# A fused attention, MLP and soft-MoE kernel: softmax over the slots at the end, row-tiled fp32 combine, smaller VectorE work, free slots handed out in any order

## Chip, cores and metric

The kernel runs on one core of a Trainium2 chip. The metric is device microseconds (us) of one execution, the median of several; smaller is better. "Engines" are PE (TensorE; PEld its weight loads), DVE (VectorE), ACT (ScalarE), POOL (GpSimd) and SP, which issues every DMA here from one queue.

## What is computed

Three layers in fp32, on 4608 tokens (8 batches of 576) of width 512. In the code `SP` = 72 pooled keys, and one *tile* is 128 tokens (36 tiles).

```
# 1 attention, 8 heads of 64, keys and values pooled by 8
k_p, v_p = mean over 8 tokens of k, v
x = softmax(q k_p^T / 8) v_p
# 2 MLP with a rational activation, 512 -> 2048 -> 512
h = x w_in;  P = a0 + a1 h + a2 h^2 + a3 h^3;  Q = 1 + |b0||h| + |b1|h^2
x = (P/Q) w_out
# 3 soft mixture of 8 experts with 4 slots each
logits = x phi                                  # 4608 x 32
slot_in = softmax over TOKENS(logits)^T x       # 32 x 512
slot_out[e] = relu(slot_in[e] w1[e]) w2[e]      # per expert, 512 -> 1024 -> 512
out = softmax over SLOTS(logits) slot_out       # 4608 x 512
```

## The kernel before

**Order of the work.** Each step of the program is an `op(engine, duration, function, reads, writes, key)`. `Plan.run` (line 146) plays a list schedule: of all steps whose inputs are there and whose buffers can be had, it takes the one that can start first by the durations written beside it, then the one with the smallest `key`. Each engine, and SP's DMA queue, then executes its instructions strictly in the order in which they were picked. `LAT = 0.12` is added where a result goes to another engine. So the constants set only the order; on the chip an instruction whose input is late holds up all that stands behind it on its engine.

**Buffers.** `Res` (line 40) is a ring of equal buffers under a tag: the next user gets the buffer that was given out longest ago, and waits for it even where another one is already free. Tags that matter here: `kv` (3, raw weights and keys/values from DMA), `t` (2, a weight matrix row block while it is rebuilt), `gt` (10, MLP activations transposed), `w` (16, the MLP's first weights), `xh` and `xl` (2 each, attention output split in a high and a low part), `h` (2, PSUM, 2 banks each) and `wk` (2, PSUM). A buffer made while `late` is set (everything of the experts and the tail) gets a slot only after all earlier users of the tag have had theirs.

**First stage.** Weights come as 64-bit numbers and are rebuilt in fp32 by `words` (line 394): a DMA to `raw`, ACT at L401, then four VectorE steps L402 to L407. `win` (line 410) then splits `w_in` into a high (ACT L416) and a low part (POOL L417). `wout` (line 420) stores the rebuilt rows to DRAM (L424), transposes them and multiplies with phi to get `wpt`, so that logits come straight from the activations. `pooling` (line 296) sums keys and values over 8 tokens on VectorE (L303 keys, 2 per batch; L310 values, 4 per batch).

**Rounds.** 9 rounds of 4 tiles. In a round, `dense` (line 449) runs over 8 pairs of 128 hidden units: 24 fp32r matmuls of 512 columns (L458 to L460) into `h`; the activation on ACT (L465 to L468, L475, L478), POOL (L469, L472, L474) and DVE (L470, L479 to L483); then `lg` (L490, logits) and `gp` (L503, transposes) on PE and copies to `gt` (L507). Beside it `attention` (line 315) prepares the next round's 4 tiles; its row sums are a reduce, an addition of 1e-9 (L355) and a reciprocal. At the end of a round `routing` (line 511) takes the maximum per slot over tokens (reduce L518, transpose L520, DVE L523 to L525, PE L528), the exponentials, rescales the running sum of slot inputs (PE L572, DVE L578), and also makes this round's softmax over slots (DVE L554 to L564, ACT L558).

**Experts and tail.** `experts` (line 586) queues the 64 weight DMAs of 512 KB (`wx`) and 16 of 256 KB. `tail` (line 620) finishes the slot inputs, runs layer one (L694) and layer two (L723), both 4 experts side by side in the four 32-column groups of PE, then the combine: slot outputs are split in a high and a low part (L761 ACT, L762 DVE), for each tile the slot weights stand four times over 128 rows (POOL L733, PE L741, ACT L749, DVE L753), and one fp32r matmul per tile (L772) gives 128 x 512 outputs, two tiles per `h` buffer. ACT copies the first tile out (L774), DVE the second (L776), and one DMA of 512 KB stores both (L777).

Of the kernel before, what the change touches and what calls it, by code (L numbers as in the profile page):

```python
# [18 lines left out]
SP = 72  # L19
# [17 lines left out]
LAT = 0.12  # L37


class Res:  # L40


    def __init__(self, pool, tag, bufs):
        self.pool, self.tag, self.bufs, self.given = pool, tag, bufs, []
        self.due = 0

    def free_at(self, late, more):
        n = len(self.given) + more
        if late and self.due:
            return None  # L50
        if n < self.bufs:
            return 0.0
        n -= self.bufs
        return self.given[n].released() if n < len(self.given) else None


class Buf:
# [13 lines left out]
    def released(self):  # L71
        return self.end if self.left == 0 else None

    def choose(self, more={}):
        best = None
        for r in self.res:
            f = r.free_at(self.late, more.get(r, 0))
            if f is not None and (best is None or f < best[0]):
                best = (f, r)
        return best  # L80

    def take(self):
        r = self.choose()[1]
        r.given.append(self)
        r.due -= not self.late
        self.t = r.pool.tile(self.shape, self.dtype, tag=r.tag, name=self.name, bufs=r.bufs)
# [12 lines left out]
class Plan:  # L99
# [46 lines left out]
    def run(self):  # L146
# [14 lines left out]
        while left:  # L161
            best = None
            for t in live:
                s0 = t.ready
                ok, more = True, {}
                for b in t.bufs:
                    if b.t is None:
# [4 lines left out]
                        more[c[1]] = more.get(c[1], 0) + 1  # L172
# [12 lines left out]
            if best is None:  # L185
                raise RuntimeError("no task can start: " + str([(t.alts[0][0], t.key, [b.name for b in t.bufs if b.t is None and b.choose() is None]) for t in live]) + str({k: [(b.name, b.left) for b in r.given[-r.bufs:]] for k, r in self.R.items()}))
            _, t, i, s = best
            e, d, fn, p = t.alts[i]
            if len(t.alts) > 1:
                for i2, (e2, d2, fn2, p2) in enumerate(t.alts):  # L190
                    s2 = max(t.ready, free[e2])
                    if e2 == "POOL":
                        s2 = max(s2, port["DVE"])
                    elif e2 == "DVE" and p2:
                        s2 = max(s2, port["POOL"])
                    if s2 + d2 < s + d:
                        e, d, fn, p, s = e2, d2, fn2, p2, s2
# [25 lines left out]
def soft_moe_kernel(ctx: ExitStack, tc: tile.TileContext, qT, kT, vP, w_in, w_out, ab, phi, w1, w2, sel, vmask, out):  # L223
# [11 lines left out]
    for tag, n in (("q", 3), ("kv", 3), ("at", 2), ("att", 1), ("st", 4), ("xh", 2), ("xl", 2), ("A", 3), ("S", 2),  # L235
                   ("U", 3), ("w", 16), ("gt", 10), ("L", 1), ("en", 1), ("m", 3), ("cs", 2), ("t", 2), ("wo", 1)):
        R[tag] = Res(sb, tag, n)
    for tag, n in (("h", 2), ("r", 1), ("wk", 2)):
        R[tag] = Res(ps, tag, n)

    late = [False]
    P.R = R
# [15 lines left out]
    call = fixed([128, NTILE, 32], "call", np_=NR)  # L258
# [6 lines left out]
    vms = fixed([128, 4], "vms")  # L265
    wpt = fixed([128, NF, 32], "wpt", np_=NF)
    den = fixed([128, 1], "den")
    mrun = fixed([1, 5, 32], "mrun")
    lgb = Fixed(ps.tile([128, 2, 128], F32, name="lg"))
    lgb.np = 2  # L270
# [9 lines left out]
    op("POOL", 0.2, lambda: g_.memset(den.t, 0.0), [], [den], -90)  # L280
    op("POOL", 0.4, lambda: g_.memset(Sacc.t, 0.0), [], [Sacc], -90)
    op("POOL", 0.2, lambda: g_.memset(mrun.t[:, 4, :], -3.0e38), [], [mrun], -90)
# [7 lines left out]
    def att_key(t):  # L290
        r, j = divmod(t, 4)
        if r == 0:
            return -8.0 + 6.0 * j
        return run_at(r - 1) + run_len(r - 1) * j / 4.0

    def pooling(b):
        need = att_key(first_tile[b])
        for i in range(2):
            key = need - 0.4 + 0.1 * i if b == 0 else need - 40 + 8 * i
# [4 lines left out]
               [t], [(o, i)], key)  # L304
        for i in range(4):
            key = need + 4 + 0.1 * i if b == 0 else need - 20 + 5 * i
            t = buf("kv", [SP, 128, 8], "vst")
# [3 lines left out]
               [t], [(o, i)], key)  # L311
# [3 lines left out]
    def attention(t):  # L315
# [6 lines left out]
        if j == 0:  # L322
            xh[r] = buf("xh", [128, 4, 512], "xh", F32R, 4)
            xl[r] = buf("xl", [128, 4, 512], "xl", F32R, 4)
# [4 lines left out]
        e = buf("at", [128, 2, 4, SP], "e", np_=2)  # L329
# [14 lines left out]
        def sub(par):  # L344
            m = st.t[:, 0, 4 * par : 4 * par + 4].rearrange("p (h o) -> p h o", o=1).to_broadcast([128, 4, SP])
            v_.tensor_tensor(out=e.t[:, par], in0=v3(par), in1=m, op=ALU.subtract)
# [4 lines left out]
        op("ACT", 0.69, lambda: a_.activation(out=e.t, in_=e.t, func=AF.Exp, scale=1.0 / 64.0), [e], [e], k0 + 4)  # L351

        def sums():
            v_.tensor_reduce(out=st.t[:, 1, :], in_=e.t.rearrange("p a h s -> p (a h) s"), axis=AX.X, op=ALU.add)
            v_.tensor_scalar_add(st.t[:, 1, :], st.t[:, 1, :], 1e-9)  # L355
# [492 lines left out]
```

## Time and profile before

| what | us |
|---|---|
| runs (3) | 1035.82, 1037.12 (median), 1042.73 |
| profiled execution, its own time | 1038.82 |
| its span, first to last instruction | 1037.0 |
| mean granted TensorE clock | 0.91 of 2.4 GHz |

In the profile a line such as L469 is a line of the kernel. Busy time of PE is modelled from pipelined starts. A row of the waits says which engine and line stood idle, and whose end released it. A row of the windows gives, for a stretch of the span, each engine's busy time with the number of instructions, the granted clock (1.00 is 2.4 GHz, 0.50 is 1.2 GHz), the busy share of the 16 DMA engines and GB/s.

### The profile page before, as it was taken

The page shows a single profiled execution, that of the slowest core. Times are in us where ns is not written, and L with a number is a line of the kernel's source. Part 1 is how long each engine was busy: PE and PEld are TensorE (multiplying, and loading weights), DVE is VectorE, ACT ScalarE, POOL GpSimd, SP SyncE. Part 2 cuts the span into 40 slices and gives each one's busy share as a digit, 9 for nine tenths or more (in the row PEclk, how much of TensorE's full clock was granted, in tenths as well). Part 3 has the DMA queues.
Part 4 walks back from the last instruction along what each step waited for, and adds up shares of the span by engine and source line. Part 5 has one row for each costly group of instructions (what it writes and reads, how often), then busy time and mean ns, then how long its engine had stood idle before and what let it go on. Part 6 is the DMA issues. An engine that isn't in the chain of part 4 may idle for free. (4 is left out here: it accounts for less than half of the span.)

```text
span 1037.0 us, 15229 instructions
## 1 busy us (share of the span) xinstructions
PE 876.4 (85%) x5939; PEld 604.6 (58%) x5939; DVE 722.2 (70%) x1142; ACT 600.2 (58%) x880; POOL 498.4 (48%) x288
## 2 busy tenths in 40 slices
PE   2785686678998998898999989999999898948995
PEld 1564565456675666666767656666676675633322
DVE  5758786777966796787778887878687658552204
ACT  1454555545666657667667666776776766652203
POOL 0143433344465755656556665665675664640000
PEclk9997768788998999999999999999999998978995
DMA  7532334432310021021002100300000052345979
GB/s 221 157 92 92 112 112 117 163 94 75 116 53 1 11 78 46 11 73 40 22 1 75 59 1 21 106 11 22 1 11 2 1 165 82 124 138 221 400 280 356
DMA packets 34151, 97.54 MB, mean 94 GB/s; under 512 B 4000, under 2 KB 4128, under 8 KB 34080
## 3 DMA queue, kind: packets, MB, share of 16 engines
q1 hardware_dynamic: 34080, 96.57, 28.1%
q8 instruction: 47, 0.77, 0.3%
q14 instruction: 24, 0.20, 0.1%
HBM read 82.92 MB, written 13.63 MB: 93 GB/s over the span
## 5 line engine op out<-in xcount | busy, mean ns | idle before, releaser
L469 POOL TENSOR_TENSOR a<-a,s 128x1024 f32<-128x1024 f32 x72 | 172.3, 2394 | 264.7 <-ACT a L467 229.4
L458 PE MATMUL h<-xh,wh 128*128 128x512 f32 x576 | 261.9, 455 | 29.7 <-ACT wh L416 14.5
L460 PE MATMUL h<-xh,wh 128*128 128x512 f32 x576 | 239.9, 417 | 1.8 <-POOL wh L417 1.6
L459 PE MATMUL h<-xl,wh 128*128 128x512 f32 x576 | 239.2, 415 | 0.2 <-DVE xl L388 0.2
L474 POOL TENSOR_TENSOR u<-u,s 128x1024 f32<-128x1024 f32 x72 | 171.7, 2385 | 5.8
L479 DVE SCALAR_TENSOR_TENSOR u<-u,r 128x512 f32<-128x512 f32 x144 | 98.1, 681 | 94.3 <-ACT r L478 93.8
L458 PEld LDWEIGHTS h<-xh,wh 128*128 128x128 f32 x576 | 116.2, 202 | 69.1 <-DVE a L470 19.2
L460 PEld LDWEIGHTS h<-xh,wh 128*128 128x128 f32 x576 | 115.9, 201 | 32.6 <-POOL wh L417 5.4
L507 ACT ACTIVATE gt<-gp 128x512 f32<-128x512 f32 x144 | 82.8, 597 | 76.4 <-PE gp L503 75.8
L459 PEld LDWEIGHTS h<-xl,wh 128*128 128x128 f32 x576 | 116.5, 202 | 17.8 <-DVE xl L388 1.0
L478 ACT ACTIVATE r<-s 128x512 f32<-128x512 f32 x144 | 86.8, 603 | 48.5 <-DVE a L483 47.1
L481 DVE SCALAR_TENSOR_TENSOR r<-a,abt,r 128x512 f32<-128x512 f32 x144 | 107.8, 749 | 0.0
L483 DVE SCALAR_TENSOR_TENSOR a<-u,r 128x512 f32<-128x512 f32 x144 | 98.8, 686 | 4.3
L470 DVE SCALAR_TENSOR_TENSOR a<-h,abt,a 128x1024 f32<-128x1024 f32 x72 | 91.9, 1277 | 12.4 <-POOL a L469 12.4
L490 PE MATMUL lg<-a,wpt 128*32 128x128 f32 x1152 | 64.1, 298 | 42.0 <-DVE a L483 40.4
L465 ACT ACTIVATE s<-h 128x1024 f32<-128x1024 f32 x72 | 73.7, 1023 | 42.4 <-PE h L460 42.1
L503 PE MATMUL gp<-ident,a 128*128 128x128 f32 x576 | 91.8, 297 | 5.1 <-DVE Sacc L578 2.3
L468 ACT ACTIVATE u<-h 128x1024 f32<-128x1024 f32 x72 | 73.6, 1022 | 37.1 <-PE h L460 36.5
L475 ACT ACTIVATE s<-u,cc 128x1024 f32<-128x1024 f32 x72 | 82.7, 1149 | 14.5 <-POOL u L474 14.4
L472 POOL TENSOR_SCALAR s<-u,gb 128x1024 f32<-128x1024 f32 x72 | 86.7, 1204 | 6.5
L467 ACT ACTIVATE a<-h,abt 128x1024 f32<-128x1024 f32 x72 | 87.1, 1209 | 0.0
L503 PEld LDWEIGHTS gp<-ident,a 128*128 128x128 f32 x576 | 70.7, 151 | 25.7 <-issue 12.3
(119 smaller groups left out, 1110.1 us busy)
## 6 DMA issues: line engine op xcount, KB each, us to landing
wx<-in_w SPq DMA_DIRECT2D x64, 512.0 KB
kst<-in_kT SPq DMA_DIRECT2D x16, 576.0 KB
qt<-in_qT SPq DMA_DIRECT2D x36, 256.0 KB
vst<-in_vP SPq DMA_DIRECT2D x32, 288.0 KB
out_dram<-o SPq DMA_DIRECT2D x18, 512.0 KB
raw<-in_w_in SPq DMA_DIRECT2D x16, 512.0 KB
raw<-in_w_out SPq DMA_DIRECT2D x16, 512.0 KB
wod<-wo SPq DMA_DIRECT2D x16, 256.0 KB
```

The source lines that it names most:

```text
L458: p_.matmul(o, w[:, 0, k], xh[r].t[:, k], start=(k == 0), stop=False)
L459: p_.matmul(o, w[:, 0, k], xl[r].t[:, k], start=False, stop=False)
L460: p_.matmul(o, w[:, 1, k], xh[r].t[:, k], start=False, stop=(k == 3))
L467: op("ACT", t_act(1024, 1, 2), lambda: a_.activation(out=fl(A), in_=fl(h), func=AF.Identity, scale=a3, bias=a2), [h, abt], [A], c)
L469: op("POOL", t_pool(1024), lambda: g_.tensor_tensor(out=fl(A), in0=fl(A), in1=fl(S_), op=ALU.mult), [S_], [A], c + 3)
L470: op("DVE", t_dve(1024, 1), lambda: v_.scalar_tensor_tensor(out=fl(A), in0=fl(h), scalar=a1, in1=fl(A), op0=ALU.mult, op1=ALU.add), [h, ab ...
L474: op("POOL", t_pool(1024), lambda: g_.tensor_tensor(out=fl(U), in0=fl(U), in1=fl(S_), op=ALU.mult), [S_], [U], c + 5)
L478: op("ACT", t_act(512, 0), lambda f=f, q=q: a_.activation(out=q.t, in_=S_.t[:, f], func=AF.Exp, scale=-1.0), [(S_, f)], [q], c + 10)
L479: op("DVE", t_dve(512), lambda f=f, q=q: v_.scalar_tensor_tensor(out=U.t[:, f], in0=U.t[:, f], scalar=QC, in1=q.t, op0=ALU.add, op1=ALU.mult),
L481: op("DVE", t_dve(512, 1), lambda f=f, q=q: v_.scalar_tensor_tensor(out=q.t, in0=A.t[:, f], scalar=a0, in1=q.t, op0=ALU.add, op1=ALU.mult) ...
L483: op("DVE", t_dve(512), lambda f=f, q=q: v_.scalar_tensor_tensor(out=A.t[:, f], in0=U.t[:, f], scalar=-2.0, in1=q.t, op0=ALU.add, op1=ALU. ...
L503: p_.transpose(pt.t[:, j, f, :], A.t[:, f, o : o + 128], ident)
```

## The change

**Slots.** A tag is now a list of separate slots; a new buffer takes whichever slot is free first. Tags gain alternatives: raw weights may lie in `kv` or `gt`, rebuilt rows in `t` or `gt`, the first values in `kv` or `gt`; `xh` and `xl` become one tag `x` with 4 slots, and 8 of the expert loads use it: four as before, and four that take the last round's two buffers (items 24 to 27).

**Plan.** A step on PE is planned 0.6 us behind its inputs (`SLACK`) instead of 0.12. Pooling may run on POOL as a tree of three additions, where that starts earlier. Round 1's attention is due later, and pooling of batch 1 too.

**VectorE.** The 1e-9 of the row sums is a 73rd element of the reduced buffer, so L355 goes. In `routing`, the running maximum is put in as a 129th column of the logits by ACT (so L524 goes), the copy over four groups goes from DVE (L525) to ACT, the update of `den` from DVE (L535) to ACT; L538 goes.

**Softmax over slots.** L554 to L564 and L558 leave the rounds; a round only copies its transposed logits (one ACT copy of 128 columns). In the tail three groups (4, 4 and 1 rounds) make maximum, difference, exponential, sum and reciprocal, then PE transposes once per round instead of four times, and ACT copies. The division moves into the output copies.

**Combine.** The slot outputs are divided (ACT), gathered to four copies by an fp32 matmul of 512 columns and copied out in two halves (ACT, DVE). Each tile is one fp32 matmul with 32 rows, tile j of a round in row group j.

**Last pair.** The last pair of the last round runs its activation in halves, and its two copies to `gt` may go to DVE.

```
-LAT = 0.12
+LAT, SLACK = 0.12, 0.6
...
-    def free_at(self, late, more):
-        n = len(self.given) + more
...
-        n -= self.bufs
-        return self.given[n].released() if n < len(self.given) else None
+    def free_at(self, i):
+        b = self.held[i]
+        return 0.0 if b is None else None if b.left else b.end
...
-                o.ready = max(o.ready, t.end + (LAT if o.alts[0][0] != e or t.nbytes else 0.0))
+                f = o.alts[0][0]
+                o.ready = max(o.ready, t.end + (0.0 if f == e and not t.nbytes else SLACK if f == "PE" else LAT))
...
+    def tree(t, o):
...
+        g_.tensor_tensor(out=t[ix(0, 4)], in0=t[ix(0, 4)], in1=t[ix(4, 8)], op=ALU.add)
+        g_.tensor_tensor(out=t[ix(0, 2)], in0=t[ix(0, 2)], in1=t[ix(2, 4)], op=ALU.add)
...
+        g_.tensor_tensor(out=o, in0=t[ix1(0)], in1=t[ix1(1)], op=ALU.add)
...
-        raw = buf("kv", [128, 512, 2], "raw", I32)
+        raw = buf(["kv", "gt"], [128, 512, 2], "raw", I32)
...
-        t = buf("t", [128, 512], "wi")
+        t = buf(["t", "gt"], [128, 512], "wi")
...
-            v_.tensor_tensor(out=mrun.t[:, 4, :], in0=mrun.t[:, 4, :], in1=mrun.t[:, 0, :], op=ALU.max)
-            v_.tensor_copy(mrun.t[:, 0:4, :], mrun.t[:, 4:5, :].to_broadcast([1, 4, 32]))
...
+        op("ACT", 0.27, lambda: a_.activation(out=mrow_.t[:, 0:4, :], in_=mrow_.t[:, 4:5, :].to_broadcast([1, 4, 32]), func=AF.Copy),
+           [(mrow_, 0)], [(mrow_, 1)], k0)
...
+        op("PE", 0.9, lambda: p_.matmul(pg.t, gsel.t, so.t, start=True, stop=True), [so, gsel], [pg], kk)
+        op("ACT", 0.4, lambda: a_.activation(out=so4.t[:, 0:256], in_=pg.t[:, 0:256], func=AF.Copy), [pg], [(so4, 0)], kk)
+        op("DVE", 0.42, lambda: v_.tensor_copy(so4.t[:, 256:512], pg.t[:, 256:512]), [pg], [(so4, 1)], kk)
...
-                op("PE", 0.25, lambda t=t, pv=pv: p_.matmul(pv(), cT[t // 16].t[:, t % 16, :], spk.t, start=True, stop=True), [(cT[t // 16], t % 16 // 4), spk], [(q, j)], kk)
...
+                for i in range(2):
+                    j = 2 * (n % 2) + i
+                    rr = slice(32 * j, 32 * j + 32)
+                    p_.matmul(po.t[:, i], cTs.t[rr, n // 2, :], so4.t[rr, :], start=True, stop=True)
```

## Rows read from the trace of the kernel before

**Rows 1.** the page, busy time, share of the span and instructions

```profile
PE 876.4 (85%) x5939; PEld 604.6 (58%) x5939; DVE 722.2 (70%) x1142; ACT 600.2 (58%) x880; POOL 498.4 (48%) x288
```

**Rows 2.** windows by stage: us, busy PE, PEld, DVE, ACT, POOL, clock, DMA share, GB/s

```profile
30.00:263.00 233.00, 175.07 (x1048) 131.81 (x1048) 176.84 (x271) 120.44 (x191) 89.15 (x54) 0.82 0.38 116
...
683.00:767.00 84.00, 80.11 (x623) 57.18 (x621) 61.28 (x104) 60.56 (x89) 53.04 (x30) 0.98 0.04 10
...
935.00:1006.00 71.00, 67.45 (x390) 23.92 (x390) 13.79 (x32) 10.40 (x21) 3.93 (x7) 0.95 0.84 326
1006.00:1037.00 31.00, 17.86 (x37) 8.46 (x36) 13.11 (x19) 11.32 (x19) 0.00 (x0) 0.57 0.83 304
```

**Rows 3.** lines on DVE, first 263 us: busy us, mean ns | idle before

```profile
L310 DVE TENSOR_REDUCE vp<-vst 72x128 f32<-72x1024 f32 x12 | 14.4, 1206 | 2.5 <-DMA vst<-in_vP 2.4
L403 DVE TENSOR_SCALAR wo<-wo 128x512 int32<-128x512 int32 x16 | 14.0, 874 | 0.5
...
L402 DVE TENSOR_SCALAR wo<-wo 128x512 f32<-128x512 f32 x16 | 10.6, 663 | 18.0 <-ACT wo L401 18.0
L342 DVE TENSOR_REDUCE st<-sc 128x4 f32<-128x288 f32 x22 | 9.3, 452 | 11.8 <-PE sc L336 11.8
...
L303 DVE TENSOR_REDUCE kp<-kst 128x144 f32<-128x1152 f32 x6 | 8.1, 1353 | 11.2 <-DMA kst<-in_kT 11.2
...
L403 DVE TENSOR_SCALAR wi<-wi 128x512 int32<-128x512 int32 x16 | 6.8, 426 | 0.5
...
L355 DVE TENSOR_SCALAR st<-st 128x8 f32<-128x8 f32 x11 | 5.6, 505 | 0.4
```

**Rows 4.** waits of SP's DMA queue, first 260 us: us, times, longest us

```profile
SPq L275 <- DVE wo L407: 96.3, 13, 13.5
```

**Rows 5.** waits of PE in the rounds, 263 to 935 us: us, times, longest

```profile
PE lg L490 <- DVE a L483: 31.3, 24, 3.4
PE h L458 <- DVE a L470: 11.6, 19, 0.9
PE pm L528 <- DVE mrun L525: 8.5, 6, 3.0
```

**Rows 6.** timeline at the end of one round, DVE: start us, us

```profile
773.95 2.24 DVE L524 TENSOR_TENSOR mrun<-mrun 1x32 f32<-1x32 f32 x1
```

**Rows 7.** the same timeline, PE

```profile
776.50 0.38 PE L528 MATMUL pm<-ident,mrun 1*128 1x1 f32 x2 [1.50 <-DVE mrun L525]
```

**Rows 8.** windows in the tail and the output stage, columns as in Rows 2

```profile
932.00:935.00 3.00, 2.77 (x17) 1.85 (x17) 0.68 (x3) 1.01 (x2) 0.00 (x0) 0.50 0.00 0
947.00:950.00 3.00, 3.00 (x30) 0.82 (x22) 0.00 (x0) 0.00 (x0) 0.00 (x0) 1.00 1.03 416
955.00:962.00 7.00, 7.00 (x66) 2.54 (x59) 0.75 (x1) 0.53 (x2) 0.43 (x1) 1.00 0.83 297
...
1011.00:1031.00 20.00, 15.37 (x30) 6.99 (x28) 10.74 (x16) 9.23 (x16) 0.00 (x0) 0.50 1.03 378
```

**Rows 9.** timeline of the output stage: start us, us, engine, line

```profile
1006.05 0.69 ACT L761 ACTIVATE shi<-lo,mf 128x512 fp32r<-128x512 f32 x1 [27.74 <-PE lo L723]
1006.77 0.75 DVE L762 SCALAR_TENSOR_TENSOR spk<-lo,mf,shi 128x512 fp32r<-128x512 f32 x1 [25.94 <-ACT shi L761]
...
1012.05 2.12 PE L772 MATMUL po<-spk,cT 128*128 128x512 f32 x4 [0.52 <-DVE o L776]
...
1013.31 0.60 ACT L774 ACTIVATE o<-po 128x512 f32<-128x512 f32 x1 [1.14 <-PE po L772]
1013.94 0.69 DVE L776 COPY o<-po 128x512 f32<-128x512 f32 x1 [1.04 <-ACT o L774]
```

**Rows 10.** the page's costliest groups, one addition of 1024 columns on POOL

```profile
L469 POOL TENSOR_TENSOR a<-a,s 128x1024 f32<-128x1024 f32 x72 | 172.3, 2394 | 264.7 <-ACT a L467 229.4
```

**Rows 11.** lines, whole span: a one-column step on ACT

```profile
L534 ACT ACTIVATE m<-mold,m 128x1 f32<-128x1 f32 x8 | 2.3, 290 | 0.0
```

**Rows 12.** the chain that ended last, in layer one: start us, us

```profile
954.75 7.07 PE l L694 x64
```

More of the change, by code (lines that the diff above doesn't have):

```diff
@@ L36, with __init__, view @@
 t_pool1 = lambda n: 0.1 + 0.0011 * n
[L37 removed]
+LAT, SLACK = 0.12, 0.6
 class Res:
[L43 to L54 removed]
+    def __init__(self, pool, tag, n, width, kept=()):
+        self.pool, self.tag, self.kept = pool, tag, kept
+        self.n, self.width, self.due, self.held = n, width, 0, [None] * n
+    def free_at(self, i):
+        b = self.held[i]
+        return 0.0 if b is None else None if b.left else b.end
+    def view(self, i, shape, dtype, name):
+        if self.kept:
+            return self.kept[i]
+        n = 1
+        for x in shape[1:]:
+            n *= x
+        assert n <= self.width
+        return self.pool.tile(shape, dtype, tag=f"{self.tag}{i}", name=name, bufs=1)
 class Buf:
@@ L62, in __init__ @@
         self.res, self.late = res, late
-        if not late:
-            for r in res:
-                r.due += 1
+        for r in res:
+            r.due += not late
         self.shape, self.dtype, self.name = shape, dtype, name
@@ L69, in __init__, with choose @@
         self.w, self.r = {}, {}
-    def released(self):
-        return self.end if self.left == 0 else None
-    def choose(self, more={}):
+    def choose(self, but=()):
         best = None
         for r in self.res:
-            f = r.free_at(self.late, more.get(r, 0))
-            if f is not None and (best is None or f < best[0]):
-                best = (f, r)
+            if self.late and r.due:
+                continue
+            for i in range(r.n):
+                if (r, i) in but:
+                    continue
+                f = r.free_at(i)
+                if f is not None and (best is None or f < best[0]):
+                    best = (f, r, i)
         return best
     def take(self):
[L83 to L86, printed above, removed]
+        _, r, i = self.choose()
+        r.held[i] = self
+        for o in self.res:
+            o.due -= not self.late
+        self.t = r.view(i, self.shape, self.dtype, self.name)
 class Fixed(Buf):
@@ L185, in run @@
             if best is None:
-                raise RuntimeError("no task can start: " + str([(t.alts[0][0], t.key, [b.name for b in t.bufs if b.t is None and b.choose() is None]) for t in live]) + str({k: [(b.name, b.left) for b in r.given[-r.bufs:]] for k, r in self.R.items()}))
+                raise RuntimeError("no task can start: " + str([(t.alts[0][0], t.key, [b.name for b in t.bufs if b.t is None and b.choose() is None]) for t in live][:40]))
             _, t, i, s = best
             e, d, fn, p = t.alts[i]
[L189 to L197, printed above, removed]
             for b in t.bufs:
@@ L463, in dense @@
         A, S_, U = (buf(x, [128, 2, 512], x.lower(), np_=2) for x in "ASU")
-        fl = lambda x: x.t.rearrange("p a b -> p (a b)")
-        op("ACT", t_act(1024), lambda: a_.activation(out=fl(S_), in_=fl(h), func=AF.Square), [h], [S_], c, after=was("sq"), also=[A, U])
-        seq("sq", P.tasks[-1])
-        op("ACT", t_act(1024, 1, 2), lambda: a_.activation(out=fl(A), in_=fl(h), func=AF.Identity, scale=a3, bias=a2), [h, abt], [A], c)
-        op("ACT", t_act(1024), lambda: a_.activation(out=fl(U), in_=fl(h), func=AF.Abs), [h], [U], c)
```

249 lines of the change are left out of this document (123 added, 126 removed).

## Prediction, made before the change was run

> **What bounds the kernel now.** I read the page first: PE is busy 85% of the span and no other engine over 70% [rows 1]. Such an average hides the stages, so the windows come next [rows 2]. They show four different limits.
>
> *First stage, to 263 us.* From 30 to 263 us PE is busy 175.07 of 233 us at a clock of 0.82, DVE 176.84 us, ACT 120.44 us: nobody is full, DVE is nearest. So I asked for DVE's lines there, with the idle time ahead of each [rows 3]. The largest removable piece is 18.0 us ahead of L402, waiting for ACT's L401, which reads the raw weights. Why L401 is late shows in the DMA queue's own waits: SP stands 96.3 us in front of loads until DVE's last rebuild step L407 has let go of a raw buffer [rows 4]. That is a shortage of slots: three `kv` buffers in a ring, two `t` buffers. SP works in order, so such a load also holds up what is queued behind it. Bound: DVE's work plus waits made by slots.
>
> *Rounds, 263 to 935 us, 84 us each.* In the round shown PE is busy 80.11 of 84 us at clock 0.98, DVE only 61.28 [rows 2]. PE is the bound, and only what makes PE wait can be won. PE's waits there: 31.3 us in 24 pieces where `lg` (L490) was put in the order before its input from L483 was done, 11.6 us where `h` waits for L470 to read the last buffer, 8.5 us in the routing chain at L528 [rows 5]. The last is seen closely in one round: L524, an operation on 32 numbers, takes 2.24 us [rows 6], and PE stands 1.50 us at L528 [rows 7].
>
> *Experts, 935 to 1006 us.* DMA share 0.84 over the stage [rows 2], 1.03 at 416 GB/s once it runs, but 0.00 at 932 to 935 us when no slot is free [rows 8]. Bound: weight loading, with a hole ahead of it.
>
> *Output, from 1006 us.* DMA share 1.03 at 378 GB/s with PE's clock at 0.50 [rows 8]: 18 stores of 0.524 MB at 378 GB/s are 1.387 us each, 25.0 us together. The computing just keeps up: one pair goes through PE from 1012.05, ACT at 1013.31 and DVE at 1013.94 to 1014.63, that is 2.58 us, with two buffers in turn, 1.29 us a pair [rows 9].
>
> **The change part by part.** All against the profiled execution, whose span is 1037.0 us.
>
> *First stage.* (a) Slots: raw and rebuilt rows can take ten more slots, so loads run ahead. I count the 18.0 us ahead of L402 as gone; between 0 (SP's order keeps them late) and -18.0. (b) DVE's 11.8 us at L342 waits for PE's scores; a plan that expects PE later and attention of round 1 due later should remove half, -5.9; between 0 and -11.8. (c) L355, 11 times here: -5.6, DVE being the bound; the 73rd element in the reduce I take as nothing. (d) Pooling: 18 reduces, 14.4 + 8.1 = 22.5 us, 1.25 us each. POOL is busy 89.15 of 233 us [rows 2], so the plan may put about half of them there: -11.2; between 0 and -22.5. What POOL pays: an addition of 1024 columns took 2394 ns [rows 10], so a tree of 576 + 288 + 144 columns is about 2.36 us (estimate by columns), nine trees 21 us. (e) What they cost DVE: L403 took 426 ns a piece on the `wi` rows and 874 ns on the `wo` rows [rows 3], the same operation, 7.2 us more for sixteen. If that is POOL's doing, more POOL work makes more of it; I take +5, between 0 and +21 (every tree blocks DVE for its whole length). The Trainium skill, "SBUF — State Buffer", section "SBUF: two separate sides", says that the port pair VectorE shares with GpSimd is an exclusive lock held for the whole instruction, the loser fully blocked; the 2.24 us of L524 [rows 6], about the length of one POOL addition [rows 10], agree. By that rule alone the term would be its upper end, +21. Sum: -18.0 - 5.9 - 5.6 - 11.2 + 5 = **-36**; ends -58 and +15.
>
> What is late next there: DVE's rebuild steps themselves, then POOL's L417.
>
> *Rounds.* DVE has time to spare, so the removed small steps are worth only what PE waits for. The 8.5 us at L528 go, since L523 now reads PSUM and an ACT copy follows. Two new one-column or 128-element steps on ACT enter the routing chain (the 129th column, the copy); such a step took 290 ns [rows 11], and can stand behind an ACT step in progress. For the 6 times that PE waited I take 0.5 us each, +3; between 0 and the old 8.5. The 31.3 us at `lg`: planning PE 0.48 us later than before puts matmuls that are ready ahead of it; I take half, -15.7, between 0 and -31.3. The 11.6 us at `h` come from buffers and stay; at best they go too. ACT gets four small steps a round and loses one, 3 x 0.29 = 0.9 us; it is busy 60.56 of 84 [rows 2], so this hides; if ACT were the bound it would be +7 in eight rounds. Sum: -8.5 + 3 - 15.7 = **-21**; ends -51 and +7.
>
> *Experts.* Four more weight tiles find a place at the end of the last round, into the hole. At 416 GB/s one takes 0.524/0.416 = 1.26 us, so the load ends 5.0 us earlier; between 0 (slots given late) and -5.0. The last pair in halves: POOL's last addition is half as long, -1.2; between 0 and -2.4. Softmax in three groups and its copies lie beside the matmuls, where DVE is busy 13.79 and ACT 10.40 of 71 us [rows 2]; 27 transposes fewer save nothing while loads are late. If that cover were gone, three groups of some four 512-column steps at about 0.7 us [rows 9] would be 8 us of DVE.
>
> *Output.* Ahead of it, L761 and L762 took 0.69 and 0.75 us [rows 9]. Now: 0.69, an fp32 matmul of 512 columns, copies. In layer one 64 instructions on four column groups took 7.07 us [rows 12] at clock 1.00 [rows 8]: two instructions a matmul, 16 per group, so 0.88 us a matmul, 1.77 at half clock. The two half copies take between 0.3 (half of ACT's 0.60, side by side) and 1.29 (0.60 + 0.69, full length, in turn) [rows 9]; I take 0.65. 0.69 + 0.88 + 0.65 + 0.2 for hand-overs = 2.4 against 1.5: +1; ends +0.4 and +1.5. Then each pair needs two fp32 matmuls. Side by side at full clock, a pair's chain lies between 0.88 + 0.69 + 0.75 = 2.32 and 3.58 us (all of the old 1.26 us ahead of ACT added), by two buffers 1.16 to 1.79; the 1.387 us of the stores would mostly cover it. At half clock PE alone needs 1.77 a pair. I take 1.53, nearer to the store rate: 18 x (1.53 - 1.387) = +2.5; ends 0 and +6.9. No row shows two 32-row matmuls at once; the nearest is the column groups of rows 12, which do run at once. One after another they cost 1.77 at full and 3.53 at half clock, up to 18 x (3.53 - 1.387) = +39. The Trainium skill, "TensorEngine Tiling (Array Packing)", section "Key Properties", says that tiles operate independently and can run matmuls in parallel; by that rule the 39 us cannot come, and rows 12 agree for columns. Sum of experts and output: -5.0 - 1.2 + 1 + 2.5 = **-3**; ends -7 and +39.
>
> Total: -36 - 21 - 3 = -60. Span 977.0; the profiled execution's own time was 1.8 us over its span, and 1.7 us above the median of the runs, so a median of **977 us**.
>
> **Rivals.**
> 1. *The first stage stays.* SP's one queue and DVE's order keep the raw loads late; idle time only changes its releaser. For it: DVE is already busy 76% there [rows 2]. Against: 96.3 us of waits on a slot [rows 4]. 977 + 36 = 1013 us.
> 2. *The rounds stay.* PE finds another late input: 977 + 21 = 998 us. For it: PE at 95% busy [rows 2]. Against: 24 separate waits with one cause [rows 5].
> 3. *The output becomes PE's.* The 32-row matmuls run one after another, at the clock of 0.50 that this stage has now [rows 8]: 977 - 2.5 + 39 = 1013 us. Against: fuller use of PE had clock 1.00 at 947 to 962 us [rows 8].
> 4. *Slower: trees ahead of the pairs.* The plan puts all 48 poolings on POOL, and a tree of 2.36 us stands in front of L469, which starts every pair's chain; L470, `h` and then PE follow late. Without the pooling gain the other terms are -60 + 11 = -49 us, so it decides once 21 trees delay PE in full; at 25 it is 1037 - 49 + 59 = 1047 us. Against: POOL stands idle 264.7 us ahead of L469, mostly for ACT [rows 10], and a tree fits in there.
> 5. *More than forecast.* Every removable wait of DVE's goes and the rounds follow: half of the way to the low ends (-58 and -51), 977 - 26 = 951, or less.
>
> **How the numbers follow.** Chances: forecast 0.42, first stage stays 0.15, rounds stay 0.12, output on PE 0.13, trees 0.08, more 0.10. The likeliest gives 977. A measurement of this kernel tells about 1% from no change. Faster by over 1% (below 1026.7) are the forecast, rival 5 and most of rivals 1 to 3: 0.83. Within 1%: the upper tails of rivals 1 and 3, 0.09. Slower: rival 4, 0.08. The range from 935 to 1030 leaves out rival 4, those tails, and the far end of rival 5.
>
> **What would show it.** Right: the wait of SP on L407 falls to under half of 96.3 us, the first round's routing comes some 30 us earlier; per round, `lg` on L483 and `pm` waits halve and a round takes 81 to 82 us; the weight DMA has no empty stretch just before layer one; the output pairs follow each other every 1.4 to 1.6 us. Wrong: the first round's end stays near 263 us; output pairs at 1.77 us or more; POOL's waits before L469 vanish while PE's waits on L470 grow well over 11.6 us.

## The result, and the profile after

The changed kernel takes **1001.91 us** (median of 4 runs, 999.06 to 1003.22), the kernel before 1038.2 us beside it: a ratio of 0.9642, 95% interval 0.9601 to 0.9683. That is 24.9 us above the forecast of 977 and inside its range. The profiled execution has a span of 997.3 us.

I cut it at the points that the prediction used: the start of the first round's `pm` transpose (end of the first stage), the same of the last round, and the end of the span.

| | before, us | after, us | difference | forecast |
|---|---|---|---|---|
| first stage | 263.0 | 247.6 | -15.4 | -36 |
| rounds | 671.4 | 645.4 | -26.0 | -21 |
| last routing to the end | 102.6 | 104.3 | +1.7 | -3 |

The page of the kernel after, part 1, which answers to [rows 1]:

```profile
PE 869.9 (87%) x5950; PEld 603.0 (60%) x5950; DVE 633.8 (64%) x1002; ACT 605.6 (61%) x906; POOL 546.1 (55%) x347
```

DVE lost 88 us and 140 instructions, POOL gained 48 us (the trees alone take 54), PE works as long as before. Windows by stage, kernel after, columns as in [rows 2]:

```profile
30.00:247.60 217.60, 167.32 (x1001) 128.09 (x999) 157.17 (x251) 115.49 (x183) 102.61 (x71) 0.80 0.37 120
674.00:753.00 79.00, 75.49 (x579) 54.53 (x577) 47.41 (x79) 55.72 (x82) 44.04 (x25) 0.96 0.03 8
893.00:961.00 68.00, 61.38 (x367) 21.79 (x366) 7.11 (x18) 7.85 (x19) 0.29 (x1) 0.94 0.78 309
961.00:997.30 36.30, 23.03 (x72) 7.96 (x72) 13.73 (x19) 12.27 (x18) 0.00 (x0) 0.56 0.70 260
```

In the first stage DVE has 20 us less to do than in [rows 2], yet it is still idle for 60 us of 217.6 (56 of 233 before), and PE's clock is no higher. In the output stage the DMA share fell from 0.83 to 0.70: the stores no longer set the pace. Where the first stage's waits went shows in SP's queue and on DVE. The waits of SP, kernel after, first 247.6 us (us, times, longest):

```profile
SPq L275 <- PE sc L348: 34.9, 8, 17.1
SPq L275 <- DVE wi L417: 33.1, 11, 8.9
SPq L434 <- DVE wi L412: 28.1, 7, 13.5
SPq L275 <- DVE vp L321: 24.9, 5, 19.2
```

Lines on DVE, same stretch (busy us, mean ns | idle before it):

```profile
L415 DVE SCALAR_TENSOR_TENSOR wo<-raw,wo 128x512 int32<-128x512 int32 x16 | 16.7, 1046 | 0.5
...
L484 DVE SCALAR_TENSOR_TENSOR a<-h,abt,a 128x1024 f32<-128x1024 f32 x10 | 12.8, 1276 | 15.1 <-POOL a L483 15.1
...
L493 DVE SCALAR_TENSOR_TENSOR u<-u,r 128x512 f32<-128x512 f32 x18 | 12.3, 683 | 16.5 <-ACT r L492 16.5
L321 DVE TENSOR_REDUCE vp<-vst 72x128 f32<-72x1024 f32 x10 | 12.1, 1208 | 1.9 <-DMA vst<-in_vP 1.9
...
L413 DVE TENSOR_SCALAR wo<-wo 128x512 int32<-128x512 int32 x16 | 6.8, 426 | 0.5
L314 DVE TENSOR_REDUCE kp<-kst 128x144 f32<-128x1152 f32 x5 | 6.7, 1340 | 5.8 <-DMA kst<-in_kT 5.6
L412 DVE TENSOR_SCALAR wo<-wo 128x512 f32<-128x512 f32 x16 | 6.7, 419 | 3.4 <-ACT wo L411 3.4
```

The 96.3 us of [rows 4] are gone (no wait on `wo` L417 of that size is left), and the 18.0 us ahead of L402 on `wo` [rows 3] are 3.4 (now L412), with 3.0 new ahead of the same step on `wi`. But DVE now stands 16.5 us ahead of L493 and 15.1 ahead of L484: the idle time has another releaser. The same two waits in the kernel before (us, times, longest):

```profile
DVE u L479 <- ACT r L478: 7.2, 4, 4.7
DVE a L470 <- POOL a L469: 6.1, 2, 3.8
```

PE's waits in the rounds, kernel after:

```profile
PE lg L504 <- DVE a L497: 16.4, 13, 4.3
PE h L468 <- DVE a L484: 8.6, 12, 1.6
```

Against [rows 5], the wait for `lg` has halved and that in the routing chain has left the list. L524 of [rows 6] no longer exists. The output stage after, timeline (start us, us):

```profile
961.37 1.14 PE L767 MATMUL po<-so,cTs 32*128 32x512 f32 x8 [0.93 <-DVE so L757]
962.55 1.27 ACT L770 ACTIVATE o<-po,csum 128x512 f32<-128x512 f32 x2 [1.69 <-PE po L767]
963.27 1.41 DVE L772 TENSOR_SCALAR o<-po,csum 128x512 f32<-128x512 f32 x2 [1.95 <-ACT o L770]
...
977.73 2.85 PE L767 MATMUL po<-so,cTs 32*128 32x512 f32 x8 [0.80 <-DVE o L772]
...
979.85 1.46 ACT L770 ACTIVATE o<-po,csum 128x512 f32<-128x512 f32 x2 [2.19 <-PE po L767]
980.58 1.52 DVE L772 TENSOR_SCALAR o<-po,csum 128x512 f32<-128x512 f32 x2 [2.13 <-ACT o L770]
...
981.38 2.85 PE L767 MATMUL po<-so,cTs 32*128 32x512 f32 x8 [0.80 <-DVE o L772]
```

At the half clock two pairs take 981.38 - 977.73 = 3.65 us, 1.83 a pair against the stores' 1.387. PE works 2.85 of these 3.65 us; then it waits until DVE has emptied the first pair, and DVE had waited until ACT had copied its half.

Of the signs that the prediction named, SP's wait on L407 and PE's on `lg` and `pm` fell about as it said, and a round takes 80.7 us on average. But the first routing came 15.4 us earlier and not some 30, the weight loads still have a hole (DMA share 0.06 and 0.15 from 896 to 902 us), and a pair takes 1.83 us, which the prediction had listed as a sign that it is wrong.

### The profile page after: what moved, and what is told of

Same layout as the page of the kernel before. It is cut to its first block, busy times and chain, and to the rows that moved or that the text cites. A ratio compares the mean times of both kernels' runs of the same rounds, so it can differ in the third digit from the quotient of the medians.

```text
span 997.3 us, 15176 instructions
## 1 busy us (share of the span) xinstructions
PE 869.9 (87%) x5950; PEld 603.0 (60%) x5950; DVE 633.8 (64%) x1002; ACT 605.6 (61%) x906; POOL 546.1 (55%) x347
## 4 chain that ended last, share of the span: by engine, by line
PE 70%; DVE 12%; ACT 11%; POOL 2%; issue 2%; DMA 1%; SPq 0%; ACTq 0%; DVEq 0%; POOLq 0%
PE h L468 14%; PE h L470 12%; PE h L469 12%; PE gp L517 6%; PE lg L504 4%; PE pss L572 3%; PE av L393 3%; PE sc L348 3%; PE lo L716 3%; PE pt L382 3%; DVE a L484 2%; ACT a L481 2%; PE po L767 2%; PE pw L448 2%; ACT u L482 2%
## 5 line engine op out<-in xcount | busy, mean ns | idle before, releaser
L483 POOL TENSOR_TENSOR a<-a,s 128x1024 f32<-128x1024 f32 (+1 forms) x73 | 172.1, 2359 | 185.7 <-ACT a L481 156.5
L468 PE MATMUL h<-xh,wh 128*128 128x512 f32 x576 | 258.1, 448 | 18.0 <-DVE a L484 10.1
L470 PE MATMUL h<-xh,wh 128*128 128x512 f32 x576 | 235.2, 408 | 0.9 <-POOL wh L427 0.9
L493 DVE SCALAR_TENSOR_TENSOR u<-u,r 128x512 f32<-128x512 f32 x144 | 98.3, 683 | 137.5 <-ACT r L492 136.8
L488 POOL TENSOR_TENSOR u<-u,s 128x1024 f32<-128x1024 f32 (+1 forms) x73 | 171.9, 2355 | 5.8
L468 PEld LDWEIGHTS h<-xh,wh 128*128 128x128 f32 x576 | 113.9, 198 | 57.7 <-DVE a L484 15.3
L470 PEld LDWEIGHTS h<-xh,wh 128*128 128x128 f32 x576 | 113.5, 197 | 30.0 <-POOL wh L427 2.8
L484 DVE SCALAR_TENSOR_TENSOR a<-h,abt,a 128x1024 f32<-128x1024 f32 (+1 forms) x73 | 92.1, 1262 | 24.1 <-POOL a L483 24.1
L479 ACT ACTIVATE s<-h 128x1024 f32<-128x1024 f32 (+1 forms) x73 | 73.8, 1013 | 45.4 <-PE h L470 45.0
L482 ACT ACTIVATE u<-h 128x1024 f32<-128x1024 f32 (+1 forms) x73 | 73.8, 1010 | 38.8 <-PE h L470 38.4
L489 ACT ACTIVATE s<-u,cc 128x1024 f32<-128x1024 f32 (+1 forms) x73 | 83.1, 1138 | 17.9 <-POOL u L488 17.7
L486 POOL TENSOR_SCALAR s<-u,gb 128x1024 f32<-128x1024 f32 (+1 forms) x73 | 87.0, 1192 | 7.2
L481 ACT ACTIVATE a<-h,abt 128x1024 f32<-128x1024 f32 (+1 forms) x73 | 87.3, 1196 | 1.1 <-PE h L470 1.1
L517 PEld LDWEIGHTS gp<-ident,a 128*128 128x128 f32 x576 | 70.6, 151 | 26.4 <-issue 12.9
```

What stands on the lines that cost most here:

```text
L468: p_.matmul(o, w[:, 0, k], xh[r].t[:, k], start=(k == 0), stop=False)
L470: p_.matmul(o, w[:, 1, k], xh[r].t[:, k], start=False, stop=(k == 3))
L481: op("ACT", t_act(n, 1, 2), lambda fl=fl: a_.activation(out=fl(A), in_=fl(h), func=AF.Identity, scale=a3, bias=a2), [pt_(h), abt], [pt_(A) ...
L483: op("POOL", t_pool(n), lambda fl=fl: g_.tensor_tensor(out=fl(A), in0=fl(A), in1=fl(S_), op=ALU.mult), [pt_(S_)], [pt_(A)], c + 3)
L484: op("DVE", t_dve(n, 1), lambda fl=fl: v_.scalar_tensor_tensor(out=fl(A), in0=fl(h), scalar=a1, in1=fl(A), op0=ALU.mult, op1=ALU.add), [pt ...
L488: op("POOL", t_pool(n), lambda fl=fl: g_.tensor_tensor(out=fl(U), in0=fl(U), in1=fl(S_), op=ALU.mult), [pt_(S_)], [pt_(U)], c + 5)
```

## The experiments

Twelve kernels. Each row gives the median of 4 runs (5 for `b_slots`), the ratio to the kernel before run beside it, and the three parts of its profiled execution.

| kernel | edit | median us | ratio, 95% | first stage | rounds | to the end |
|---|---|---|---|---|---|---|
| after | | 1001.9 | 0.960 to 0.968 | 247.6 | 645.4 | 104.3 |
| `a_noslack` | plan: PE steps 0.12 us behind their inputs | 984.0 | 0.945 to 0.949 | 228.6 | 648.8 | 104.3 |
| `a_notree` | no pooling on POOL | 983.3 | 0.944 to 0.948 | 234.6 | 644.0 | 104.6 |
| `a_nogt` | no spare slots | 991.6 | 0.950 to 0.957 | 233.6 | 654.4 | 104.8 |
| `a_dead` | slot softmax put back, unused | 1013.5 | 0.970 to 0.980 | 251.4 | 657.5 | 104.9 |
| `a_lat14` | plan alone (`LAT` 0.14 for 0.12) | 994.3 | 0.954 to 0.960 | 238.6 | 649.5 | 103.9 |
| `a_slack5` | plan alone (`SLACK` 0.5 for 0.6) | 990.4 | 0.949 to 0.958 | 227.2 | 652.2 | 105.5 |
| `a_none3` | the first three together | 984.3 | 0.943 to 0.952 | 242.6 | 637.3 | 102.9 |
| `b_slots` | before, with separate slots | 1027.1 | 0.984 to 0.993 | 240.8 | 680.5 | 103.4 |
| `a_split` | output pair in two tiles | 1000.0 | 0.960 to 0.966 | 249.0 | 648.2 | 104.8 |
| `a_third` | third pair of banks | 996.0 | 0.956 to 0.961 | 247.1 | 648.4 | 98.8 |
| `a_split_third` | both | 995.5 | 0.956 to 0.961 | 250.3 | 645.5 | 97.5 |
| `a_best` | `a_notree` + `a_third` | 976.6 | 0.937 to 0.944 | 236.8 | 638.6 | 98.6 |

How steady these parts are can be read from the table: after, `a_split`, `a_third` and `a_split_third` run the same order up to the output, and so do `a_notree` and `a_best`. `a_dead` runs the order of after up to the first cut. Within one order the first stage differs by at most 4.3 us and the rounds by at most 5.4, the last routing's start (the sum of both) by at most 4.2. Between orders differences are far larger. These are profiled executions; the runs of one kernel spread by 1.4 us (`a_none3`) to 12.9 us (`a_dead`, 1006.5 to 1019.4), and the profile of `a_slack5` is of its fastest run, 3.7 us under its median. An order can also move matmuls of round 1 across the cut, so the sum of the first two columns is safer than either.

**Three parts, each undone alone.** In `a_noslack`, `a_notree` and `a_nogt`:

```
-LAT, SLACK = 0.12, 0.6
+LAT, SLACK = 0.12, 0.12
```
```
-   [], [t, (o, i)], key, alt=[("POOL", 2.8, lambda t=t, o=o, i=i: tree(...), True)])
+   [], [t, (o, i)], key)
...
```
```
-        raw = buf(["kv", "gt"], [128, 512, 2], "raw", I32)
+        raw = buf("kv", [128, 512, 2], "raw", I32)
...
-        t = buf(["t", "gt"], [128, 512], "wi")
+        t = buf("t", [128, 512], "wi")
...
```

`SLACK` is the time by which a step on PE is planned behind its inputs; the expectations speak of it as a delay behind a matmul task, which is the wrong side of the step.

> The kernel after, but the planner again counts 0.12 us, not 0.6 us, between the end of a matmul task and a reader on another engine (its order alone can change). Theory: the larger figure is what halved PE's wait for `lg`. Then the 16.4 us of that wait go back to about 31, the rounds from 645 to about 660 us, the whole to about 1018 us. Rival: the order comes out much the same, and the rounds became shorter because DVE has less to do; then 1002 us, give or take 4, and the `lg` wait stays near 16.

> The kernel after without the choice of POOL for pooling: all of it on DVE, as before. Theory: the trees take work from the engine that sets the first stage; without them the stage is 7 to 11 us longer (247.6 to 255 or more), the whole 1009 to 1013 us. Rival: DVE's idle time in the stage was 70 us after and 68 before, so it is not DVE's work that sets it; then the stage moves under 3 us and the whole stays at 999 to 1005 us.

> The kernel after with its three kinds of staging tile (the index words, the two weight stagings) and the pooled values kept in their old slots, without the ten spare slots. Theory: the spare slots are what took SP's 96.3 us of waiting in the first stage away and with it 11.6 us of DVE's waits for weight loads (18.0 to 6.4); the stage grows by 10 to 18 us, the whole is 1012 to 1020 us. Rival: the waits only change their name, as DVE's idle sum shows (68 and 70 us); then under 4 us, 1000 to 1006 us.

Theories and rivals missed alike: all three became faster, by 17.9, 18.7 and 10.3 us, most of it in the first stage. Two of these runs say something that does not hang on the size of the gain. Windows of the whole first stage, first the kernel after, then `a_notree`:

```profile
0.00:247.60 247.60, 181.71 (x1091) 139.56 (x1091) 177.56 (x284) 124.46 (x197) 114.43 (x92) 0.83 0.44 145
```

```profile
0.00:234.60 234.60, 180.23 (x1138) 140.34 (x1139) 191.89 (x296) 129.26 (x203) 98.91 (x69) 0.88 0.46 153
```

Without the trees DVE has 14.3 us *more* to do and the stage ends 13 us *earlier*. Its pooling there, lines on DVE of `a_notree`:

```profile
L321 DVE TENSOR_REDUCE vp<-vst 72x128 f32<-72x1024 f32 x16 | 18.9, 1201 | 1.1 <-DMA vst<-in_vP 1.1
...
L314 DVE TENSOR_REDUCE kp<-kst 128x144 f32<-128x1152 f32 x8 | 10.7, 1342 | 6.0 <-DMA kst<-in_kT 5.9
```

That is 29.6 us against the 18.8 of the kernel after. So the trees take 10.8 us off DVE, and between these two orders nothing comes of it. In `a_noslack` PE's wait for `lg` in the rounds was 19.3 us, not 31, so most of its fall does not come from the planner's larger delay:

```profile
PE lg L504 <- DVE a L497: 19.3, 16, 3.8
```

**The old slot softmax put back.** `a_dead` runs it on a scratch tile in each round, nine times:

```
+        op("DVE", 0.6, cmax, [tp], [cs, dead], k0 + 1)
+        op("ACT", 0.3, lambda: a_.activation(out=c, in_=c, func=AF.Exp), [], [dead], k0 + 2)
...
+        op("DVE", 0.95, csm, [], [cs, dead], k0 + 20)
```

> The kernel after with the old slot softmax of every round put back as work without a use: six small VectorE operations and one exponential on a scratch tile, nine times. Theory: they stand on DVE, which feeds the next matmuls of a round, and cost most of their time: 8 to 14 us, 1010 to 1016 us. Rival: DVE is idle a quarter of a round, the operations are taken up there, and the whole stays within 3 us of 1002.

The theory's number came: +11.6 us, in the rounds +12.1, the only kernel with the change whose median lies above 1002 us. Its reason is shown for a part only. Lines on DVE of `a_dead`, from 251 to 909 us:

```profile
L583 DVE TENSOR_TENSOR dead<-dead,cs 128x128 f32<-128x128 f32 x8 | 7.0, 873 | 0.3
...
L581 DVE TENSOR_SCALAR cs<-cs 128x4 f32<-128x4 f32 x8 | 5.1, 635 | 0.3
...
L574 DVE TENSOR_TENSOR dead<-ptr,cs 128x128 f32<-128x128 f32 x8 | 2.3, 291 | 0.3
L573 DVE TENSOR_REDUCE cs<-ptr 128x4 f32<-128x128 f32 x8 | 2.3, 290 | 10.5 <-PE ptr L562 8.6 <-ACT en L566 1.4 <-ACT cTs L567 0.5
L580 DVE TENSOR_REDUCE cs<-dead 128x4 f32<-128x128 f32 x8 | 2.3, 282 | 2.8 <-ACT dead L577 2.7
...
L582 DVE RECIPROCAL cs<-cs 128x4 f32<-128x4 f32 x8 | 1.4, 178 | 0.3
```

These are 20.4 us of DVE's time. Up to the fourth round's `pm` transpose `a_dead` runs the order of after, but for three matmuls that come 16 instructions earlier, so there the operations can be priced without a change of order. Windows of these three rounds and of the rest, first the kernel after, then `a_dead`:

```profile
247.60:499.90 252.30, 241.17 (x1793) 175.19 (x1793) 173.26 (x275) 180.10 (x262) 174.20 (x106) 0.97 0.11 33
499.90:893.00 393.10, 362.63 (x2631) 258.52 (x2629) 262.12 (x408) 280.89 (x413) 257.22 (x149) 0.95 0.17 58
```

```profile
251.40:506.60 255.20, 240.28 (x1793) 172.89 (x1793) 181.47 (x293) 180.92 (x265) 173.85 (x106) 0.97 0.11 33
506.60:908.90 402.30, 366.12 (x2630) 262.10 (x2628) 271.11 (x437) 282.19 (x418) 259.16 (x152) 0.94 0.18 57
```

In the three rounds DVE has 8.2 us more to do and the time is 2.9 us longer; the other three kernels with this order took 252.3 to 254.0 us there, so 1 to 3 us reach the end. At that rate eight rounds would lose 3 to 8 us (an estimate). The other 9.2 us stand where the order has become another one too, and the two are not told apart.

**The output stage.** The three kernels keep the order of everything ahead of it.

```
-            o = buf(["w", "gt"], [128, 2, DM], "o", np_=2)
+            oa, ob = [buf(["w", "gt"], [128, DM], "o") for _ in range(2)]
```
```
-            po = buf("h", [128, 2, 512], "po", np_=2)
+            if n % 3 == 2:
+                pw_ = [buf("wk", [128, 512], "po") for _ in range(2)]
...
```

> The kernel after with the output pair in two tiles and two stores of 256 KB, so that DVE's copy has no tile in common with ScalarE's; the order of all work ahead of the output is unchanged. Theory: the copy of the second half stands behind the first for no need (18.1 us of DVE's waiting for `o`), and a pair of row tiles takes 1.83 us because matmuls, copy and copy follow one another; with the copies side by side a pair takes about 1.45 us, the output stage 29 to 31 us instead of 35.9, the whole 995 to 997 us. Rival: 32-row matmuls at the half clock set the pace (2.85 us of PE for two pairs, 1.43 each, and the start of the next): a gain of 0 to 2 us, 1000 to 1002 us.

> The kernel after with a third pair of PSUM banks in the output stage (each third pair takes the two banks that the transposes leave free); the order ahead of it is unchanged. Theory: PE waits for banks after every two pairs, which is what keeps 2.85 us of matmuls and 0.8 us of wait in a step of 3.65 us; with three pairs in flight the step is bounded by PE or by the stores, 1.40 to 1.45 us a pair: 6 to 7 us less, 995 to 996 us. Rival: the copies, one behind the other in one tile, set the pace: 1.7 us a pair or more, 1000 to 1002 us.

> Both edits of the output stage together. If each removes the same chain, together no more than the better one: 994 to 996 us, with the stores at 1.39 us a pair as the new bound. If the half clock alone sets the pace, 1000 us or more.

`a_split` missed: two output tiles change nothing (1000.0 us; the stage takes 37.2 us from the first `po`, 35.9 after). The rival's number came, but not its reason: PE still waits for DVE's copy. DVE's copy still starts the moment ACT's ends, though they have no output in common. Timeline of `a_split`:

```profile
981.32 1.35 ACT L770 ACTIVATE o<-po,csum 128x512 f32<-128x512 f32 x2 [2.30 <-PE po L767]
982.04 1.41 DVE L772 TENSOR_SCALAR o<-po,csum 128x512 f32<-128x512 f32 x2 [2.24 <-ACT o L770]
```

What they still share is the PSUM tile `po`, of which each reads one half. `a_third` has both cases in one trace: pairs on one `po` tile, and each third pair on two separate PSUM tiles, with one output tile for both copies. Timeline of `a_third` (a line of x2 or x3 is that many copies one after another; the last two lines are the third pair's, its DVE copy being the third of the x3 above):

```profile
976.25 1.35 ACT L777 ACTIVATE o<-po,csum 128x512 f32<-128x512 f32 x2 [1.27 <-PE po L774]
...
976.97 2.07 DVE L779 TENSOR_SCALAR o<-po,csum 128x512 f32<-128x512 f32 x3 [1.58 <-ACT o L777]
...
977.94 0.69 ACT L777 ACTIVATE o<-po,csum 128x512 f32<-128x512 f32 x1 [0.34 <-PE po L774]
...
978.30 0.74 DVE L779 TENSOR_SCALAR o<-po,csum 128x512 f32<-128x512 f32 x1
```

In the third pair DVE starts at 978.30, 0.33 us before ACT ends at 978.63, into the same output tile. So the two copies go in turn when they read one PSUM tile, and not because they write one output tile. The traces do not say whether the chip or the program's own ordering of that tile asks for it.

The third pair of banks is worth 6.0 us (1001.91 to 995.95), as the theory had it; that the copies of each third pair overlap comes with the same edit and is not told apart from it. Windows of the output stage, first after, then `a_third`, then `a_split_third`:

```profile
965.00:985.00 20.00, 15.26 (x46) 5.07 (x42) 8.25 (x11) 8.25 (x12) 0.00 (x0) 0.52 0.85 314
```

```profile
964.00:986.00 22.00, 21.21 (x72) 9.60 (x64) 12.07 (x18) 12.12 (x18) 0.00 (x0) 0.50 0.86 315
```

```profile
964.00:982.00 18.00, 14.07 (x72) 5.88 (x72) 12.51 (x18) 11.52 (x18) 0.00 (x0) 1.00 0.86 323
```

With three pairs in flight all 72 matmul instructions take 22 us at the half clock, 1.22 us a pair, less than the stores' 1.387. With both edits the clock stayed at 1.00 in the profiled execution, the matmuls were through in 18 us, and the whole was no faster: the stores end last either way.

**Is it the order?** After the first three misses a second theory was needed: every edit makes the planner find another order, and the one of after is a poor one. Two kernels change the order and no part (`LAT` 0.14; `SLACK` 0.5), one undoes the three parts together.

> The kernel after with the planner's small delay between engines at 0.14 us instead of 0.12 us: the same work and the same choices, in another order. The three kernels that undid one part each were 10 to 19 us faster than after, whatever they undid, and nearly all of it stood in the first stage (247.6 us after; 228.6, 234.6 and 233.6 in them). New theory: the order that the planner happened to find for the first stage of after is a poor one, the time of that stage moves by 10 to 20 us with any change of the plan, and the three parts as such are worth little; then this kernel too has a first stage of 228 to 240 us and a time of 982 to 995 us. Rival: the parts undone cost what was measured; then this kernel, which has them all, stays at 998 to 1006 us.

> The kernel after with the planner's figure behind a matmul task at 0.5 us instead of 0.6 us: a second change of the order alone, with all parts in place. Theory (an order found by luck): a first stage of 228 to 240 us, the rounds at 640 to 655 us, the whole 982 to 998 us. Rival (0.6 us is costly by itself in proportion, 18.6 us for 0.48 us): a sixth to a fifth of the gain, 997 to 1001 us.

> The kernel after with three parts undone together: no pooling on POOL, no spare slots for the stagings, 0.12 us behind a matmul task in the plan. What is left of the change is the output, the token softmax at the end, the merged small operations, and slots handed out one by one. Each of the three undone alone gave 10 to 19 us. Theory (an order found by luck): undoing all three gives about what one gave, 980 to 995 us, since none is worth much by itself. Rival (each costs its own amount): the gains add up, 18.6 + 17.9 + 10.3, to about 955 to 965 us.

994.3 and 990.4 us, the first stage 238.6 and 227.2 (0.8 below the range named): in both the new theory's numbers came, with all parts in place. For `a_none3` its range came too (984.3), and the rival, that the gains add up to 955 to 965, fell. The first `pm` transposes of after and of `a_lat14` (the last figures are first and last start):

```profile
L541 PE MATMUL pm<-ident,m x9: 269/272/379, 247.6 to 893.0; 128*1 128x128 f32 x9
```

```profile
L541 PE MATMUL pm<-ident,m x9: 270/272/379, 238.6 to 888.1; 128*1 128x128 f32 x9
```

So 8 and 12 us come from nothing but another plan: another order, and in it 24 (`a_lat14`) and 21 (`a_slack5`) poolings on POOL instead of 22. The clock alone does not explain it: over the first stage 0.86 was granted in `a_lat14` (238.6 us) and also in `a_split`, which has the order of after (249.0 us). Whether the rest (7 to 11 us of the 18.7 in `a_notree`) is a cost of those parts is not settled: there are three orders with all parts (990 to 1002) and four without some (983 to 992), and they touch. None of the three parts is shown to gain anything.

**Slots alone, in the kernel before.**

```
-    def __init__(self, pool, tag, bufs):
-        self.pool, self.tag, self.bufs, self.given = pool, tag, bufs, []
+    def __init__(self, pool, tag, n, width, kept=()):
...
```

> The kernel before with one part of the change alone: every slot a tile of its own that is handed out as it comes free, instead of tags that go round. Theory: the slots that go round are behind part of SP's 96.3 us of waiting and DVE's 18.0 us; the first stage is 5 to 15 us shorter, the whole 1022 to 1032 us. Rival: with the same number of slots under each tag the freest one is the next in turn anyway, and only the order changes: 1033 to 1042 us, to either side.

1027.1 us (ratio 0.988), inside the theory's range: the first stage is 22.2 us shorter, the rounds 9.1 longer. This is one order as well, so the gain is not shown to be that of the slots. SP's wait for L407 [rows 4] went only from 96.3 to 74.1. PE's waits in its rounds:

```profile
PE lg L497 <- DVE a L490: 30.8, 23, 5.2
PE h L465 <- DVE a L477: 10.6, 19, 0.8
```

Both are as in [rows 5]. In the kernels with the rest of the change the wait for `lg` was 14.6 us (`a_nogt`) to 21.9 (`a_lat14`), 20.0 in `a_dead`, 19.3 in `a_noslack`. A large part of it stands in the last 22 us of the last round; there, first in the kernel before, then after:

```profile
PE lg L490 <- DVE a L483: 13.1, 6, 3.4
```

```profile
PE lg L504 <- DVE a L497: 9.6, 5, 4.3
```

Elsewhere it was 18.2 us before, 16.4 in `b_slots` and 6.8 after. What cuts the whole by a third to a half is thus neither the slots, nor the 0.6 us, nor the slot softmax alone. Left are the merged operations of routing and attention, the last pair in halves and the later attention, which I did not try one by one.

**The best of both.**

> The kernel after without pooling on POOL (983.25 us) and with the third pair of PSUM banks in the output stage (worth 5.96 us in the kernel after); the order ahead of the output is that of the kernel without pooling on POOL. Theory: the output stage stands behind everything else, so its gain adds: 976 to 978 us, from the last round's routing to the end 98 to 99 us instead of 104.6. Rival: at another clock history the stores or PE take the gain back: 981 us or more.

976.6 us, ratio 0.9404 (0.9373 to 0.9436): the gain of the output stage adds, as it must where nothing stands behind it.

## Why the prediction was right, and where it was wrong

The time lies inside a range 95 us wide. Of the 24.9 us between it and the forecast, 20.6 stand in the first stage, and there chance had a part: the same parts in the order of `a_slack5` give -35.8.

**The first stage was mis-sized: -15.4 for -36.** The single terms came in part, the sum did not. (a) The idle time ahead of L402 fell by 14.6 us of the 18.0 on `wo`, by 11.6 with `wi`; (b) the wait for the scores by 3.6 (11.8 to 8.2 at L354), forecast 5.9; (c) L355 is gone; (d) against `a_notree` the trees took 10.8 us off DVE, forecast 11.2, but DVE's own pooling fell only from 22.5 us [rows 3] to 18.8, since 24 poolings instead of 18 now come before the cut. And DVE's idle time in the stage stayed, 68 us before and 70 after: other waits took the place, as rival 1 said of the releasers. The step that failed is the bound, "DVE's work plus waits made by slots": `a_notree` adds 14.3 us of DVE's work and gains 13, in another order. What the stage costs goes with the order, 227 to 250 us in three orders with all parts in place (though the order of 227 does 45 of 1091 matmul instructions later); which chains meet in it, I did not trace.

(e) The +5 had the wrong sign. The eight groups of rebuild steps on DVE took 91.1 us before and 81.7 after (without the trees 84.9), with more work on POOL: L403 on `wo` fell from 874 ns [rows 3] to 426 (now L413). That POOL slows these steps is right. Of their 128 executions 18 before and 15 after took over 1.15 times the fastest of their group, each with POOL at work, and each ended 0.28 us (L402, L403) or 0.55 us (L405, L407) behind the end of a POOL instruction; what the groups took beyond their fastest sums to 21.0 us before and 12.6 after. But how often the two meet depends on the order, and `Plan.run` plans no POOL step beside one of these (they are marked `port=True`), before as after. So nine trees do not bring nine delays, as the +21 assumed. One such meeting in `a_dead`, L583 on DVE and the POOL instruction beside it:

```profile
682.48 2.34 DVE L583 TENSOR_TENSOR dead<-dead,cs 128x128 f32<-128x128 f32 x1
```

```profile
682.29 2.37 POOL L489 TENSOR_TENSOR u<-u,s 128x1024 f32<-128x1024 f32 x1
```

L583 took 0.29 us the five times that POOL was idle at its start, and 1.16 (three times) or 2.34 us where POOL was at work; L574, which has one of its two inputs in PSUM, took 0.29 us beside POOL too. The Trainium skill, "SBUF — State Buffer", section "SBUF: two separate sides", states an exclusive lock for the whole instruction, between GpSimd and those VectorE operations that have two SBUF inputs or run in a 2-port mode. These rows agree; the +21 left out that condition.

**The rounds, -26 for -21, were right in size and half right in reason.** The wait for `lg` fell by 14.9 us, I had 15.7; but I gave it to the planner's 0.6 us, and `a_noslack` shows 19.3 us without it. "DVE has time to spare, so the removed small steps are worth only what PE waits for" priced the slot softmax at nothing; in the three rounds of `a_dead` with the order of after, 1 to 3 of its 8.2 us reach the end. The 8.5 us at L528 went, as forecast, and the wait for `h` fell by 3.0.

**The tail, +1.7 for -3.** From the last routing to the end of the last layer -6.1, I had -6.2. Ahead of the first output pair +1.3, I had +1. The pairs: +6.5 for +2.5, and this term was mis-sized by two steps. "At half clock PE alone needs 1.77 a pair" is wrong: four row groups of two pairs overlap, 8 instructions in 1.14 us at full clock and 2.85 at half. And I divided a pair's chain by two buffers without the turn of the copies, which [rows 9] already showed (DVE at 1013.94, when ACT was done at 1013.91). One chain at half clock is PE to ACT 2.12, ACT 0.73, DVE and hand-over 0.80: 3.65 us, by two buffers 1.83.

**The rivals.** Rival 1 came halfway; its price, 36 us, was 21 in this order (20 to 24 in its repeats) and 0 to 16 in six others of the table. Rival 2 did not come. Rival 3 did not come: row tiles run side by side. The Trainium skill, "TensorEngine Tiling (Array Packing)", section "Key Properties", says that they can, and 1.14 us for four matmuls agrees. Rival 4 did not come: 22 trees run on POOL, one above the number from which I let it decide, and PE's wait for `h` fell to 8.6 us instead of growing.

**What the gain is made of,** by the start of the last routing: 934.4 us before; 921.3 with the slots alone (-13.1); 893.0 to 897.2 after. With the slot softmax put back it is 908.9 (`a_dead`), 12 to 16 us of the second step, of which the softmax itself would be 3 to 8 by the rounds in the same order. The rest of both steps, the slots, the merged operations and the order, is not told apart. The output stage gives 6.5 us back.

## What to carry to other kernels

Where a planner lays out the order, one measurement of an edit is a draw: change a harmless constant two or three times and see how far the time moves before a gain or a loss is given to the edit, or compare only the stretch in which both kernels still run the same order. Idle time of an engine counts as removable only if that engine's work, changed alone, moves the end of the stage; here 14 us more work on the "nearest" engine came, in another order, with a shorter stage. At the end of a kernel, where nothing can hide anything, count the chain of one buffer with all its hand-overs and divide by the buffers; a third buffer was worth 6 us there at no cost.

## What was not expected of the hardware

Four 32-row fp32 matmuls of 512 columns in different row groups (eight instructions) took 1.14 us at clock 1.00; at 0.50 a stream of such pairs took 1.22 us a pair when no bank was missing, with PE busy 21.21 of 22 us; in `a_split_third` the clock stayed at 1.00 with PE busy 14.07 of 18. Two engines that read different halves of one PSUM tile read in turn, whether by the chip or by the program's ordering is open; from two PSUM tiles they overlapped. The same VectorE operation on two SBUF tiles took 0.29 us, or up to 2.34 us beside a POOL instruction. In the profiled executions one order reaches the last routing within 4.2 us of 897, while three plans with the same parts reach it at 893.0, 888.1 and 879.4 us.
